# A speech joint network's forward and backward pass: 16 rows of x columns with a copied halo, x rows in one tile, and sums over u two halves at a time

## The chip, the core and the metric

The kernel runs on one core of a Trainium2 chip. The core has TensorE (PE, matmuls and their weight loads), VectorE (DVE), ScalarE (ACT), GpSimd (POOL) and SyncE (SP, which here only issues DMAs), each with its own instruction queue that is worked off in order. SBUF is the on-chip memory, PSUM the place where matmuls leave their sums. The metric is the device time of one launch in microseconds (us).

## The reference

Two batches of 16000 frames with 256 channels go through two convolutions of three taps, each followed by GELU and by taking every second frame, so that 4000 frames are left in each batch. A joint network adds each of them to each of 8 rows of `g` and takes tanh. The kernel returns the output and the gradients of all seven inputs, in bfloat16.

```python
h = sum(einsum("btc,cd->btd", xp[:, i:i+T], w1[i]) for i in range(3))   # xp: x padded by one frame at both ends
h = gelu(h)[:, ::2, :]
f = sum(einsum("btc,cd->btd", hp[:, i:i+T1], w2[i]) for i in range(3))
f = gelu(f)[:, ::2, :]
fe = einsum("btd,de->bte", f, w_f)
ge = einsum("bud,de->bue", g, w_g)
j = tanh(fe[:, :, None, :] + ge[:, None, :, :])
out = einsum("btud,dv->btuv", j, w_o)                                    # [2, 4000, 8, 256]
# returned: out and, from grad_out, the gradients of x, w1, w2, g, w_f, w_g, w_o
```

## The kernel before

The 8000 frames that are left (both batches one after the other) are cut into 17 chunks: one of 256, fifteen of 512, one of 64. A chunk of 512 lies in SBUF as 4 blocks of 128 columns: frame 4p + a of the chunk is column p of block a. Channels are in two halves of 128 (`KT` = 2, index `kt`, `mt` or `d2`). The batches meet inside chunk 8, whose operations therefore come in two segments.

A chunk goes through three stages.

- `stage_a` (lines 532 to 591): x arrives with channels on partitions in tile `XC`, which has one slot. A chunk of 512 needs 17 rows of columns: 16 of its own and row 0, the frame before each group of 16 (the halo), which is row 16 of the column to its left. `load_xc` (line 395) fetches them with four transposing DMAs of 5, 4, 4 and 4 rows. Convolution, GELU and its derivative follow (`conv_gelu`, line 494) for odd frames (`HTo`, `G1o`), even frames (`HTe`, `G1e`) and the second layer (`FT`, `G2`). In `conv_gelu` PE writes PSUM tiles `ps`; ACT makes `g_sq` (L505) and the GELU (L507); DVE makes `g_s` (L510) and so gives the PSUM tile back; L519 to L529 make the derivative. Then `FE` = f w_f in its transposed layout, and the row layouts `FER`, `HRo`, `HRe`, `FR` for the weight gradients.
- `stage_j` (line 622): for each of four pairs of u, ACT makes `JT` = tanh(FE + ge) (L638) and DVE and ACT the same in rows, `JR`, from `FER` and the broadcast rows `GEB` (L662, L667). PE makes the output from JT, the gradient of w_o from JR and `GO` (into `GWO`), and from `GOT` (grad_out transposed) the gradient of the joint sum into `ps`. `JSQ` is the square of JT. For each u and half DVE computes (JSQ - 1) x ps into `NGZ` (L709, with a sum along the row for the gradient of ge), and adds it to `ZS` (L724); for the last u the sum goes to `NGFE` (L722). `NGZ` is a 512-wide fp32 tile for one half and has two slots.
- `stage_de` (line 767): the backward pass of the two layers (`GF`, `GHe`, `GHo`, with their halos copied by POOL, L377 and L383), the row layouts `NFR`, `GFR`, `GHeR`, `GHoR` (class "rows", three slots), the weight gradients (`wgrad`, added to accumulators in L763) and the gradient of x (`GX`). `load_x` (line 444) brings x in rows for the gradient of w1, in two tiles of 9 rows for a chunk of 512.

While chunk k is in `stage_j`, chunk k+1 is in `stage_a` and chunk k-1 in `stage_de`. The order on each engine isn't that of the text: a planner (`Flow.issue`, line 107) walks through a simulated time, and at each step places the operation that can start first, by costs written at each operation and a due time (`at`, or `F.now`). An operation that needs a new tile (`new=`) is placed only when its class has a free slot; the classes and their numbers of slots are in lines 295 to 298, and most give slots out in the order of the text. `ps` has 7 slots in PSUM. The matmul of GOT and WOT asks for its `ps` tile and for its `NGZ` tile (line 690). The planner's order is fixed at build time; on the chip semaphores keep the dependences.

All DMAs but a few at the start are issued on SP's queue, where an issue waits for its own data and holds what is behind it.

Of the kernel before, what the change touches and what calls it, by code (L numbers as in the profile page):

```python
# [220 lines left out]
def kernel(  # L221
# [38 lines left out]
    sizes.append(NP - sum(sizes))  # L260
    assert sum(sizes) == NP

    TRANS = (0,)

    class Chunk:
# [100 lines left out]
    def zero(ap, w, new=(), at=None):  # L366
        op("POOL", 150.0, lambda e: nc.gpsimd.memset(ap(), 0.0), w=w, new=new, at=at)
# [17 lines left out]
    def row_ap(t, row, step, m, n):  # L385
        return bass.AP(tensor=t.tensor, offset=t.offset + row * D, ap=[[step * D, m], [1, n * D]])
# [8 lines left out]
    def load_xc(k, at, behind=()):  # L395
        c = chunks[k]
        A, Pw = c.A, c.Pw
        XC = st[k]["XC"] = buf("xc", [P, 4 * NB + 1, KT, P], BF16, "XC")
        cuts = [1, 4 * A + 1] if c.first else [0] + [4 * n + 1 for n in range(1, A + 1)]
        for n, (lo, hi) in enumerate(zip(cuts, cuts[1:])):  # L400
            dma("SP", lambda lo=lo, hi=hi: XC[:, lo:hi, :, :Pw].rearrange("p r k c -> p (r k) c"),
                lambda lo=lo, hi=hi: row_ap(x_, 4 * c.c0 - 1 + lo, 4 * A, Pw, hi - lo), r=[], w=[(XC, ("m", n))],
                bytes_=Pw * (hi - lo) * D * 2 * 1.3, new=[XC] if n == 0 else [], transpose=True, at=at, behind=behind, sub="xc")
        if c.first:
            op("POOL", 330.0, lambda e: nc.gpsimd.tensor_copy(out=XC[:, 0, :, 1:Pw], in_=XC[:, 4 * A, :, 0:Pw - 1]),
               r=[(XC, ("m", 0))], w=[(XC, "h")], at=at)
            zero(lambda: XC[:, 0, :, 0:1], [(XC, "h")], at=at)
        if c.px is not None:
            zero(lambda: XC[:, 0, :, c.px:c.px + 1], [(XC, ("m", 0))], at=at)

    def load_go(k, up, at, after=()):
        c = chunks[k]
# [31 lines left out]
    def load_x(k, at, after=()):  # L444
        c = chunks[k]
        A = c.A
        tiles = []
        for h in range((A + 1) // 2):
            nb = min(2, A - 2 * h)
            nr = 4 * nb + 1  # L450
            X = buf("xc" if c.last else "x", [P, 9, D], BF16, "X")
            row = 4 * c.c0 - 3 + 8 * h
            lo, new = 0, [X]
            if c.first and h == 0:
                op("POOL", 150.0, lambda e, X=X: nc.gpsimd.memset(X[0:1, 0:3], 0.0), w=[(X, "a")], new=new, at=at, after=after)
                new = []
                dma("SP", lambda X=X, nr=nr: X[0:1, 3:nr], lambda nr=nr: x[0:1, 0:nr - 3, :], r=[], w=[(X, "b")],
                    bytes_=(nr - 3) * 512, at=at, after=after)
                dma("SP", lambda X=X, nr=nr: X[1:16, 0:nr].rearrange("p f d -> p (f d)"),
                    lambda row=row, nr=nr: row_ap(x_, row + 4 * A, 4 * A, 15, nr), r=[], w=[(X, "c")],  # L460
                    bytes_=15 * nr * 512, at=at, after=after)
                lo = 16
            rd = []
            if c.last and h == 0:
                p0 = c.Pw // 32 * 32
                zero(lambda X=X, p0=p0: X[p0:c.Pw + 1], [(X, "z")], new=new, at=at)
                new, rd = [], [(X, "z")]
                dma("SP", lambda X=X: X[c.Pw:c.Pw + 1, 0:3], lambda: x[B - 1:B, T - 3:T, :], r=rd, w=[(X, "b")],
                    bytes_=1536, at=at, after=after)
            dma("SP", lambda X=X, lo=lo, nr=nr: X[lo:c.Pw, 0:nr].rearrange("p f d -> p (f d)"),  # L470
                lambda row=row, lo=lo, nr=nr: row_ap(x_, row + 4 * A * lo, 4 * A, c.Pw - lo, nr),
                r=rd, w=[(X, "m")], bytes_=(c.Pw - lo) * nr * 512, new=new, at=at, after=after)
            tiles.append(X)
        return tiles
# [147 lines left out]
    def stage_j(k, t0, dt, GEB):  # L622
# [5 lines left out]
        def pair(up):  # L628
# [51 lines left out]
            for step in range(4):  # L680
# [21 lines left out]
                if first:  # L702
                    Z, zap = (ZS, d2), lambda d2=d2: ZS[:, d2, :W]
                else:
                    Z, zap = NGZ, lambda NGZ=NGZ: NGZ[:, :W]

                def stt(e, d2=d2, ps=ps, u=u, zap=zap, JSQ=JSQ):
                    for _, lo, hi, si in c.segs:
# [3 lines left out]
                            accum_out=NGP[:, d2, u, si:si + 1])  # L712
                op("DVE", sum(c_dve((s[2] - s[1]) * A) + 6 for s in c.segs), stt,
                   r=[JSQ, ps], w=[Z, (NGP, (d2, u, k))])
                if not first:
                    if fin_ and d2 == 0:
                        S["NGFE"] = buf("ngfe", [P, NB, KT, P], BF16, "NGFE")

                    def zadd(e, d2=d2, NGZ=NGZ, fin_=fin_):
                        a, b = ZS[:, d2, :W], NGZ[:, :W]  # L720
                        if fin_:
                            nc.vector.tensor_tensor(out=S["NGFE"][:, 0:A, d2, :Pw], in0=fl(a, A), in1=fl(b, A), op=ALU.add)  # L722
                        else:
                            nc.vector.tensor_tensor(out=a, in0=a, in1=b, op=ALU.add)  # L724
# [42 lines left out]
    def stage_de(k, t0, dt):  # L767
# [158 lines left out]
                    put(Pw, Pw + 1, 0, 3)  # L926
        for i in range(KK):
            def xl(da):
                return lambda a, m, d2: X[a // 2][:m, 4 * (a % 2) + da, d2 * P:(d2 + 1) * P]
# [3 lines left out]
            wgrad(ACC1, i, lambda i=i: ACC1[:, i],  # L933
                  [(xl(i), rr(GHoR), c.sblk, X + [GHoR]),
                   (xl(i + 2), he, c.sblk, [GHeR] + ([GHzR] if GHzR is not None else []))], out_2[i])
            tick()

    def store(dst, src, r, scale=None):
# [73 lines left out]
    xh = st[0]["XC"].log[-1][0]  # L1012
# [25 lines left out]
    def wt(dst, src, n, at, behind):  # L1038
        dma("SP", lambda: dst[:], lambda: src, r=[], w=[dst], bytes_=n * 131072, transpose=True, at=at, behind=behind)


    def part(k):
        return str(k) if k < 4 else "e" if k >= NG - 2 else "s"
# [7 lines left out]
    for k in range(NG + 1):  # L1051
        c = chunks[min(k, NG - 1)]
        t0, Wk = (c.t0, float(c.W)) if k < NG else (float(NP), 300.0)
        if k < NG:
            F.stage = part(k)
            for up in range(1 if c.last else UP):
                load_go(k, up, t0 + Wk * (up / UP - 0.7), [xh] if k == 0 else [])
                load_got(k, up, t0 + Wk * (up / UP - 0.5))
        F.stage = part(k)
        if k + 1 < NG:  # L1060
            load_xc(k + 1, t0 - Wk * 0.3, [st[0]["GOT"][1].log[0][0]] if k == 0 else [])
        if k == 0:
            fr = st[1]["XC"].log[-1][0]
# [55 lines left out]
```

## Time and profile before

| what | before |
|---|---|
| median of 3 runs | 806.55 us (805.66 to 807.43) |
| the profiled execution | 807.35 us |
| its span, first to last instruction | 805.6 us |
| granted TensorE clock | 1.000 |
| PE busy | 780.1 us (97%), 5916 matmuls |
| DVE busy | 727.5 us (90%), 1626 instructions |
| ACT busy | 732.0 us (91%), 1175 instructions |
| POOL busy | 61.4 us (8%), 179 instructions |
| moved by DMA | 180.86 MB |

The span runs from the first to the last instruction; what the profiled execution has over it (1.75 us) lies outside. A busy time is the time in which at least one instruction of the engine was running, and a group's mean is the length of one instruction, which may overlap the next one's start. A wait is counted at the engine that stood still, with what released it.

### The profile page before, as it was taken

What the parts mean: (1) busy time and instruction counts of PE and PEld (TensorE: products, weight loads), DVE (VectorE), ACT (ScalarE), POOL (GpSimd) and SP (SyncE); (2) the same over time, 40 slices, a digit from 0 to 9 for tenths busy, and PEclk for the clock granted to TensorE, in tenths of its full rate; (3) what the DMA queues carried; (4) which work ended last, traced back from release to release, by engine and by line L of the source; (5) the groups of instructions that cost most, each with busy time, mean ns of one, the idle gap of its engine ahead of it and who ended that gap; (6) DMA issues with size and microseconds to landing.
All of it is one profiled execution on the core that took longest, in us unless ns stands there. A gap on an engine that the chain in (4) does not pass through costs nothing. (4 is left out here: it accounts for less than half of the span.)

```text
span 805.6 us, 16179 instructions
## 1 busy us (share of the span) xinstructions
PE 780.1 (97%) x5916; PEld 558.7 (69%) x5916; DVE 727.5 (90%) x1626; ACT 732.0 (91%) x1175; POOL 61.4 (8%) x179
## 2 busy tenths in 40 slices
PE   7879999999999999999999999999999999999996
PEld 6546668576675766767677686776767767677865
DVE  4799999998998989989899898998989989899974
ACT  5999999999999989998999999999999999998742
POOL 2100000100001001010000101000010000103010
PEclk9999999999999999999999999999999999999999
DMA  9998999999999999998999999999999999997984
GB/s 191 208 203 209 218 277 220 234 237 232 240 219 222 251 236 222 214 239 208 239 232 210 262 218 231 221 247 254 217 225 243 241 212 221 239 249 190 249 168 130
DMA packets 387940, 180.86 MB, mean 225 GB/s; under 512 B 311794, under 2 KB 379668, under 8 KB 387860
## 3 DMA queue, kind: packets, MB, share of 16 engines
q1 hardware_dynamic: 386916, 179.16, 99.0%
q8 instruction: 46, 0.75, 0.4%
q10 hardware_dynamic: 784, 0.39, 0.2%
q0 software_dynamic: 160, 0.27, 0.1%
q14 instruction: 34, 0.28, 0.1%
HBM read 52.40 MB, written 50.34 MB: 128 GB/s over the span
## 5 line engine op out<-in xcount | busy, mean ns | idle before, releaser
L638 ACT ACTIVATE JT<-FE,GE 128x512 bf16<-128x512 bf16 (+4 forms) x288 | 182.4, 690 | 0.2
L709 DVE SCALAR_TENSOR_TENSOR NGZ<-JSQ,ps 128x512 f32<-128x512 bf16 (+3 forms) x252 | 150.1, 608 | 1.0 <-PE ps L335 0.6
L335 PE MATMUL ps<-WO,JT 128*128 128x256 bf16 (+1 forms) x1008 | 146.2, 273 | 2.7 <-DVE NGZ L709 1.7
L335 PE MATMUL ps<-GOT,WOT 128*128 128x512 bf16 (+2 forms) x544 | 146.3, 362 | 2.2 <-DVE g_s L510 1.0
L344 ACT CAST OUT_SB<-ps 128x512 bf16<-128x512 f32 (+1 forms) x207 | 122.7, 606 | 18.3 <-PE ps L335 18.1
L667 ACT ACTIVATE JR<-JR 128x1024 bf16<-128x1024 bf16 (+1 forms) x124 | 130.7, 1071 | 5.7 <-DVE JR L662 5.6
L335 PEld LDWEIGHTS <-JT 128*128 128x128 bf16 (+1 forms) x1008 | 98.1, 98 | 51.5 <-issue 4.5
L696 ACT ACTIVATE JSQ<-JT 128x1024 bf16<-128x1024 bf16 (+2 forms) x124 | 127.3, 1027 | 7.2 <-DVE NGZ L709 5.1
L335 PE MATMUL GWO<-GO,JR 128*128 128x256 bf16 (+1 forms) x1008 | 130.7, 273 | 1.5 <-ACT JR L344 0.8
L724 DVE TENSOR_TENSOR ZS<-ZS,NGZ 128x512 f32<-128x512 f32 (+2 forms) x204 | 129.1, 638 | 0.4
L335 PEld LDWEIGHTS <-JR 128*128 128x128 bf16 (+1 forms) x1008 | 97.5, 98 | 23.5 <-ACT JR L667 2.6
L510 DVE SCALAR_TENSOR_TENSOR g_s<-g_sq,ps 128x512 bf16<-128x512 bf16 (+2 forms) x102 | 65.1, 640 | 41.7 <-ACT HTo L507 41.1
L335 PEld LDWEIGHTS <-W 128*128 128x128 bf16 x612 | 58.5, 99 | 61.0 <-issue 4.6
L335 PE MATMUL ps<-XC,W 128*128 128x512 bf16 (+2 forms) x408 | 85.5, 367 | 1.9 <-DMA XC<-in_x_dram 1.2
L662 DVE TENSOR_TENSOR JR<-FER,GEB 128x1024 bf16<-128x1024 bf16 (+1 forms) x124 | 83.3, 678 | 3.0 <-PE GWO L335 2.3
L335 PEld LDWEIGHTS <-X 128*128 128x128 bf16 (+1 forms) x756 | 73.8, 98 | 9.7 <-issue 0.4
L763 DVE TENSOR_TENSOR ACC<-ACC,ps 128x512 f32<-128x512 f32 x90 | 60.1, 680 | 19.3 <-PE ps L335 18.8
L335 PE MATMUL ps<-W1T,GHo 128*128 128x256 bf16 (+1 forms) x378 | 72.2, 273 | 0.2
L335 PEld LDWEIGHTS <-WOT 128*128 128x128 bf16 x544 | 51.9, 98 | 29.1 <-issue 4.1
L335 PE MATMUL ps<-W1T,GHe 128*128 128x256 bf16 (+1 forms) x376 | 71.8, 273 | 0.0
L505 ACT ACTIVATE g_sq<-ps 128x512 bf16<-128x512 f32 (+2 forms) x102 | 59.6, 586 | 10.2 <-PE ps L335 10.0
L346 ACT ACTIVATE GX_SB<-ps 128x512 bf16<-128x512 f32 (+1 forms) x101 | 60.1, 616 | 5.6 <-PE ps L335 4.6
(137 smaller groups left out, 1109.8 us busy)
## 6 DMA issues: line engine op xcount, KB each, us to landing
GO<-in_grad_out_dram SPq DMA_DIRECT2D x60, 512.0 KB, 5.0
out_dram<-OUT_SB SPq DMA_DIRECT2D x60, 512.0 KB, 5.1
X<-in_x_dram SPq DMA_DIRECT2D x30, 576.0 KB, 5.4
out_dram<-GX_SB SPq DMA_DIRECT2D x30, 512.0 KB, 5.0
GO<-in_grad_out_dram SPq DMA_DIRECT2D x5, 256.0 KB, 4.2
GOT<-GO SPq DMA_TRANSPOSE x65, 4.9
out_dram<-OUT_SB SPq DMA_DIRECT2D x4, 256.0 KB, 3.1
XC<-in_x_dram SPq DMA_TRANSPOSE x62, 4.7
```

The costliest lines, as they stand in the source:

```text
L335: nc.tensor.matmul(ps_ap, lhsT=lhsT, rhs=rhs, start=start, stop=stop)
L344: nc.scalar.copy(out=dst(), in_=src())
L346: nc.scalar.activation(out=dst(), in_=src(), func=ACT.Copy, scale=scale)
L505: op("ACT", c_act(W, True), lambda e, mt=mt, ps=ps: nc.scalar.activation(out=sq[:, 0:A, mt, :Pw], in_=fl(ps[:, :W], A), func=ACT.Square, s ...
L510: op("DVE", c_dve(W), lambda e, mt=mt, ps=ps: nc.vector.scalar_tensor_tensor(out=s[:, 0:A, mt, :Pw], in0=sq[:, 0:A, mt, :Pw], scalar=1.0, ...
L638: nc.scalar.activation(out=fl(JT[:, j, mt, :W], A)[:, :, lo:hi], in_=FE[:, 0:A, mt, lo:hi], func=ACT.Tanh, bias=GE[:, b, mt, 2 * up + j:2 ...
L662: op("DVE", c_dve(n * 2 * D, 0.5), lambda e, lo=lo, n=n, m=m, JR=JR: nc.vector.tensor_tensor(out=JR[:m, 0:n], in0=S["FER"][:m, lo:lo + n]. ...
L667: op("ACT", c_act(n * 2 * D), lambda e, n=n, m=m, JR=JR: nc.scalar.activation(out=JR[:m, 0:n], in_=JR[:m, 0:n], func=ACT.Tanh), r=[JR], w= ...
L696: nc.scalar.activation(out=JSQ[:, :, :W], in_=JT[:, j, :, :W], func=ACT.Square)
L709: nc.vector.scalar_tensor_tensor(out=fl(zap(), A)[:, :, lo:hi], in0=fl(JSQ[:, d2, :W], A)[:, :, lo:hi], scalar=1.0, in1=fl(ps[:, :W], A)[: ...
L724: nc.vector.tensor_tensor(out=a, in0=a, in1=b, op=ALU.add)
L763: op("DVE", c_dve(512), lambda e: nc.vector.tensor_tensor(out=acc_ap().rearrange("p k d -> p (k d)"), in0=acc_ap().rearrange("p k d -> p ( ...
```

## The change

- `load_xc`: a chunk's transposing DMAs now bring rows 1 to 16 in four pieces of 4 rows. Row 0 is made in SBUF by POOL: 127 columns copied from row 16 of the same tile, and column 0 from `XCh`, a small tile of two slots into which POOL copies the last column of row 16 for the next chunk. The first chunk did the first of these copies already.
- `load_x`: x rows come in one tile of 17 rows with one DMA (first chunk: three, last chunk: two); the class "x" has one slot of 17 rows where it had two of 9.
- Sums over u: `NGZ` holds both halves (1024 wide, two slots). The two L709 instructions of a u write its halves, and one add of 1024 columns follows the second. For the last u two adds of 512 remain, in one operation behind the second half.
- `geb` gets a second slot. Classes with fewer slots: `fe` 2 to 1, `got` 4 to 3, `hro` 2 to 1, `rows` 3 to 2, `x` 2 to 1.
- `F.shift` is set to an empty table, which is what it was by default, and the operations that waited for "the last entry of XC's log" now name the last XC DMA itself.

```diff
-    for name, n in (("xc", 1), ("hto", 2), ("hte", 1), ("ft", 1), ("g1o", 2), ("g1e", 2), ("g2", 2), ("fe", 2),
-                    ("fer", 2), ("gsq", 2), ("gs", 2), ("jt", 3), ("go", 3), ("got", 4), ("out", 3), ("jr", 3),
-                    ("hro", 2), ("hre", 2), ("fr", 2), ("jsq", 2), ("ngz", 2), ("ngfe", 1), ("gf", 2), ("gho", 1),
-                    ("ghe", 1), ("rows", 3), ("x", 2), ("gx", 3), ("ghh", 2), ("geb", 1)):
+    for name, n in (("xc", 1), ("hto", 2), ("hte", 1), ("ft", 1), ("g1o", 2), ("g1e", 2), ("g2", 2), ("fe", 1),
+                    ("fer", 2), ("gsq", 2), ("gs", 2), ("jt", 3), ("go", 3), ("got", 3), ("out", 3), ("jr", 3),
+                    ("hro", 1), ("hre", 2), ("fr", 2), ("jsq", 2), ("ngz", 2), ("ngfe", 1), ("gf", 2), ("gho", 1),
+                    ("ghe", 1), ("rows", 2), ("x", 1), ("gx", 3), ("ghh", 2), ("xch", 2), ("geb", 2)):
...
-        cuts = [1, 4 * A + 1] if c.first else [0] + [4 * n + 1 for n in range(1, A + 1)]
+        cuts = [1, 4 * A + 1] if c.first else [1] + [4 * n + 1 for n in range(1, A + 1)]
...
+        end = (XC, ("m", len(cuts) - 2))
+        op("POOL", 330.0, lambda e: nc.gpsimd.tensor_copy(out=XC[:, 0, :, 1:Pw], in_=XC[:, 4 * A, :, 0:Pw - 1]),
+           r=[end], w=[(XC, "h")], at=at)
         if c.first:
...
             zero(lambda: XC[:, 0, :, 0:1], [(XC, "h")], at=at)
+        else:
+            xh_ = st[k - 1]["XCh"]
+            op("POOL", 200.0, lambda e: nc.gpsimd.tensor_copy(out=XC[:, 0, :, 0:1], in_=xh_[:]), r=[xh_], w=[(XC, "h")], at=at)
...
+        if not c.last:
+            xh2 = st[k]["XCh"] = buf("xch", [P, KT, 1], BF16, "XC_halo")
+            op("POOL", 200.0, lambda e: nc.gpsimd.tensor_copy(out=xh2[:], in_=XC[:, 4 * A, :, Pw - 1:Pw]),
+               r=[end], w=[xh2], new=[xh2], at=at)
...
-        for h in range((A + 1) // 2):
-            nb = min(2, A - 2 * h)
-            nr = 4 * nb + 1
-            X = buf("xc" if c.last else "x", [P, 9, D], BF16, "X")
-            row = 4 * c.c0 - 3 + 8 * h
+        nr = 4 * A + 1
+        X = buf("xc" if c.last else "x", [P, 4 * NB + 1, D], BF16, "X")
+        row = 4 * c.c0 - 3
...
-                NGZ = buf("ngz", [P, CW], FP32, "NGZ") if u else None
-                op("PE", c_pe([W] * KT), gj, r=[GOT, WOT], w=[ps], new=[ps, NGZ] if u else [ps])
+                if u and d2 == 0:
+                    NGZ = buf("ngz", [P, KT, CW], FP32, "NGZ")
+                op("PE", c_pe([W] * KT), gj, r=[GOT, WOT], w=[ps], new=[ps, NGZ] if u and d2 == 0 else [ps])
...
-                if not first:
-                    if fin_ and d2 == 0:
+                if not first and d2 == KT - 1:
+                    if fin_:
...
-                    def zadd(e, d2=d2, NGZ=NGZ, fin_=fin_):
-                        a, b = ZS[:, d2, :W], NGZ[:, :W]
+                    def zadd(e, NGZ=NGZ, fin_=fin_):
+                        a, b = ZS[:, :, :W], NGZ[:, :, :W]
...
-                    op("DVE", c_dve(W), zadd, r=[(ZS, d2), NGZ], w=[(S["NGFE"] if fin_ else ZS, d2)],
-                       new=[S["NGFE"]] if fin_ and d2 == 0 else [])
+                    op("DVE", KT * c_dve(W) if fin_ else c_dve(KT * W), zadd, r=[ZS, NGZ],
+                       w=[(S["NGFE"], 0), (S["NGFE"], 1)] if fin_ else [ZS], new=[S["NGFE"]] if fin_ else [])
```

More of the change, by code (lines that the diff above doesn't have):

```diff
@@ L261 @@
     assert sum(sizes) == NP
+    SHIFT = {}
     TRANS = (0,)
@@ L446, in load_x @@
         A = c.A
-        tiles = []
-        for h in range((A + 1) // 2):
-            nb = min(2, A - 2 * h)
-            nr = 4 * nb + 1
-            X = buf("xc" if c.last else "x", [P, 9, D], BF16, "X")
-            row = 4 * c.c0 - 3 + 8 * h
[L453 to L473, printed above, removed]
@@ L474, in load_x @@
-        return tiles
+        nr = 4 * A + 1
+        X = buf("xc" if c.last else "x", [P, 4 * NB + 1, D], BF16, "X")
+        row = 4 * c.c0 - 3
+        lo, new = 0, [X]
+        if c.first:
+            op("POOL", 150.0, lambda e, X=X: nc.gpsimd.memset(X[0:1, 0:3], 0.0), w=[(X, "a")], new=new, at=at, after=after)
+            new = []
+            dma("SP", lambda X=X, nr=nr: X[0:1, 3:nr], lambda nr=nr: x[0:1, 0:nr - 3, :], r=[], w=[(X, "b")],
+                bytes_=(nr - 3) * 512, at=at, after=after)
+            dma("SP", lambda X=X, nr=nr: X[1:16, 0:nr].rearrange("p f d -> p (f d)"),
+                lambda row=row, nr=nr: row_ap(x_, row + 4 * A, 4 * A, 15, nr), r=[], w=[(X, "c")],
+                bytes_=15 * nr * 512, at=at, after=after)
+            lo = 16
@@ new lines, in load_x @@
+        rd = []
+        if c.last:
+            p0 = c.Pw // 32 * 32
+            zero(lambda X=X, p0=p0: X[p0:c.Pw + 1, 0:nr], [(X, "z")], new=new, at=at)
+            new, rd = [], [(X, "z")]
+            dma("SP", lambda X=X: X[c.Pw:c.Pw + 1, 0:3], lambda: x[B - 1:B, T - 3:T, :], r=rd, w=[(X, "b")],
+                bytes_=1536, at=at, after=after)
+        dma("SP", lambda X=X, lo=lo, nr=nr: X[lo:c.Pw, 0:nr].rearrange("p f d -> p (f d)"),
+            lambda row=row, lo=lo, nr=nr: row_ap(x_, row + 4 * A * lo, 4 * A, c.Pw - lo, nr),
+            r=rd, w=[(X, "m")], bytes_=(c.Pw - lo) * nr * 512, new=new, at=at, after=after)
@@ L476, in rows @@
+        return X
     def rows(k, cls, name, SRC, lo, n, r, at=None, pe=0):
@@ L704, in pair @@
                 else:
-                    Z, zap = NGZ, lambda NGZ=NGZ: NGZ[:, :W]
+                    Z, zap = (NGZ, d2), lambda NGZ=NGZ, d2=d2: NGZ[:, d2, :W]
                 def stt(e, d2=d2, ps=ps, u=u, zap=zap, JSQ=JSQ):
@@ L714, in pair @@
                    r=[JSQ, ps], w=[Z, (NGP, (d2, u, k))])
-                if not first:
-                    if fin_ and d2 == 0:
+                if not first and d2 == KT - 1:
+                    if fin_:
                         S["NGFE"] = buf("ngfe", [P, NB, KT, P], BF16, "NGFE")
-                    def zadd(e, d2=d2, NGZ=NGZ, fin_=fin_):
-                        a, b = ZS[:, d2, :W], NGZ[:, :W]
+                    def zadd(e, NGZ=NGZ, fin_=fin_):
+                        a, b = ZS[:, :, :W], NGZ[:, :, :W]
                         if fin_:
-                            nc.vector.tensor_tensor(out=S["NGFE"][:, 0:A, d2, :Pw], in0=fl(a, A), in1=fl(b, A), op=ALU.add)
+                            for d in range(KT):
+                                nc.vector.tensor_tensor(out=S["NGFE"][:, 0:A, d, :Pw], in0=fl(ZS[:, d, :W], A),
+                                                        in1=fl(NGZ[:, d, :W], A), op=ALU.add)
                         else:
                             nc.vector.tensor_tensor(out=a, in0=a, in1=b, op=ALU.add)
-                    op("DVE", c_dve(W), zadd, r=[(ZS, d2), NGZ], w=[(S["NGFE"] if fin_ else ZS, d2)],
-                       new=[S["NGFE"]] if fin_ and d2 == 0 else [])
+                    op("DVE", KT * c_dve(W) if fin_ else c_dve(KT * W), zadd, r=[ZS, NGZ],
+                       w=[(S["NGFE"], 0), (S["NGFE"], 1)] if fin_ else [ZS], new=[S["NGFE"]] if fin_ else [])
                 for tb, m in c.blk:
@@ L933, in stage_de @@
             wgrad(ACC1, i, lambda i=i: ACC1[:, i],
-                  [(xl(i), rr(GHoR), c.sblk, X + [GHoR]),
-                   (xl(i + 2), he, c.sblk, [GHeR] + ([GHzR] if GHzR is not None else []))], out_2[i])
+                  [(xl(i), rr(GHoR), c.sblk, [X, GHoR]),
+                   (xl(i + 2), he, c.sblk, [X, GHeR] + ([GHzR] if GHzR is not None else []))], out_2[i])
             tick()
@@ L1039, in wt @@
         dma("SP", lambda: dst[:], lambda: src, r=[], w=[dst], bytes_=n * 131072, transpose=True, at=at, behind=behind)
+    F.shift = SHIFT
     def part(k):
@@ L1062 @@
         if k == 0:
-            fr = st[1]["XC"].log[-1][0]
+            fr = st[1]["XCl"]
             wt(WFT, w_f[:, :], 1, W0 * 0.6, [fr])
```

10 lines of the change are left out of this document (4 added, 6 removed).

## The prediction

> **What bounds the kernel now.** I read the page's busy shares first, then the busy time by stretches, the chain of waits on TensorE (PE), the groups by form, and last the timeline around one chunk change. From the page, PE's busy tenths in 40 slices last:
>
> ```profile
> PE 780.1 (97%) x5916; PEld 558.7 (69%) x5916; DVE 727.5 (90%) x1626; ACT 732.0 (91%) x1175; POOL 61.4 (8%) x179
> PE   7879999999999999999999999999999999999996
> ```
>
> PE is busy in every slice but the first three and the last. The stretches (us, then busy time and instructions of each engine):
>
> ```profile
> 32.00:104.00 72.00, 65.08 (x449) 41.68 (x448) 71.10 (x161) 70.32 (x110) 6.03 (x19) 1.00 1.01 214
> 104.00:700.00 596.00, 590.77 (x4424) 423.48 (x4423) 550.70 (x1168) 567.82 (x877) 39.36 (x116) 1.00 1.03 231
> 700.00:805.60 105.60, 97.36 (x839) 73.69 (x837) 88.96 (x241) 71.84 (x142) 11.36 (x28) 1.00 0.80 200
> ```
>
> Columns are PE, weight loads, VectorE (DVE), ScalarE (ACT), GpSimd (POOL). So there are two regimes. From 32 to 104 us DVE is busy for 71.1 of 72 us and PE for only 65.1: DVE sets the pace. From 104 to 700 us PE does, idle for 5.2 of 596 us. What ends its waits there (total us, times, longest), from the chain of waits between 100 and 700 us:
>
> ```profile
> PE ps L335 <- DVE g_s L510: 2.3, 6, 0.6
> PE ps L335 <- ACT FT L507: 1.0, 3, 0.4
> PE ps L335 <- DVE NGZ L709: 0.6, 3, 0.2
> ```
>
> No row has a DMA in it. In 32 to 104 us the same view gives 5.1 us of PE waits ended by DVE (g_s 1.9 and 0.7, NGZ 1.7, GF 0.6, GHe 0.2; nine waits). A change to DVE counts only through these 8.0 us; a change to DMA counts only if it makes a wait that is not there today.
>
> **The change, part by part.** First the sums over u. The groups by form (count, busy us, mean ns) and two adds in a row in the timeline (start, us):
>
> ```profile
> L724 DVE TENSOR_TENSOR ZS<-ZS,NGZ 128x512 f32<-128x512 f32 x180 | 121.9, 681 | 0.1
> ...
> 214.45 1.28 DVE L724 TENSOR_TENSOR ZS<-ZS,NGZ 128x512 f32<-128x512 f32 x2
> ```
>
> Two adds back to back take 1.28 us though one lasts 0.68, so the second starts 0.60 us after the first. The 256-wide form lasts 418 ns, so an element costs (681 - 418)/256 = 1.03 ns and a 1024-wide add lasts 0.68 + 512 x 1.03 = 1.21 us. One merged add saves 1.28 - 1.21 = 0.07 us. L724 stands 204 times (6 values of u, 2 halves, 17 chunks), so 102 merges save 7.1 us of DVE's 727.5. The last add of a chunk (L722) stays two instructions; both now wait for the second half, but at 769.07 and 793.01 us both already stand behind it: nothing. [...]
>
> What of 7.1 us reaches PE? In 32 to 104 us DVE is the bound and has 20 of these adds: 10 x 0.07 = 0.7 us, all of it. Between 100 and 700 us the nine waits above each have about one merge before them in the same unbroken DVE stream: 9 x 0.07 = 0.6 us. The pair tile also changes the order: the planner may place the matmul of GOT and WOT only when an NGZ slot is free, and with two 512-wide slots that ties it to the add of the u just before; with two slots of a pair it may run one u further ahead. No row shows that. Its bounds are a gain of what is left of those waits (2.9 - 0.6 = 2.3 us) and the loss of rival C; I take 1.0 us of gain, since the nearest rows (the waits on NGZ and g_s) are just this matmul waiting for DVE. Together: 2.3 us.
>
> Next, the 48 new POOL copies (16 chunks, three each). The halo copy of the same shape lasts 394 ns and the one-column copies some 190 ns, so POOL gets 16 x 0.78 = 12 us more on 61. Where they hide: in the chunk whose x columns are read from 198.9 us the last transpose is issued by 189.3 and should have landed near 192.5, and POOL does nothing between 161.4 (G1o's halo) and 194.29 (GF's). Queued behind them are GF's and GHe's halos (to 198.5) and HTo's (203.0), for which the next matmuls of those chunks wait. If the cover went (columns that land late), two of HTe's six taps and these halos would stand still for the delay, 0.8 us a chunk for the copies alone; PE's waits on POOL in the old run are one of 0.7 us, so I take 0. But they are not free for DVE:
>
> ```profile
> 160.23 0.80 POOL L377 COPY G1o<-G1o 128x254 bf16<-128x254 bf16 x1 [6.21 <-DVE G1o L529]
> 160.69 0.62 DVE L521 TENSOR_SCALAR g_sq<-g_sq 128x1024 bf16<-128x1024 bf16 x1
> ...
> L521 DVE TENSOR_SCALAR g_sq<-g_sq 128x1024 bf16<-128x1024 bf16 x45 | 21.5, 478 | 0.5
> L525 DVE TENSOR_SCALAR g_sq<-g_sq 128x1024 bf16<-128x1024 bf16 x45 | 18.8, 418 | 0.1
> ```
>
> The copy takes 0.80 instead of 0.39 us and the tensor_scalar under it 0.62 instead of 0.41; over the run L521 loses 45 x 60 ns = 2.7 us to such meetings, and L527 (431 ns) 0.6. That is 3.3 us for some 113 copies, 0.03 each, so 48 more cost DVE 1.4 us; at the rate at which DVE time reached PE above, 2.3/7.1, that is 0.5 us; I take 0.3, since the new copies come outside the tensor_scalar bursts.
>
> Fewer bytes: 15 rows of x columns and 15 of x rows (64 KB each) less of 180.86 MB, and 15 issues less on SyncE's queue. PE waits for no DMA after start: 0, bounds 0 and 0.
>
> Fewer slots cost only where the old order used the last slot. GOT: no transpose was issued sooner than 4.1 us after the last read of the tile three before it: 0. X: one 17-row load may start when the last X is read; the old loads started at least 5.9 us after that, and the second of each pair landed some 16 to 20 us before use: 0. HRo: now loaded where its successor was (515.34 us), over 40 us before its read: 0; the last one moves from 751.2 to 781.9 us, lands within 5 us, read at 796.4: 0. Rows of the gradients and FE:
>
> ```profile
> 508.85 3.16 SPq L359 DMA_TRANSPOSE GHeR<-GHe  x1
> 511.09 1.04 PE L335 MATMUL ps<-NFR,FR 128*128 128x256 bf16 x8
> ...
> 413.40 1.15 ACT L344 CAST FE<-ps 128x512 bf16<-128x512 f32 x2
> 420.13 0.92 ACT L638 ACTIVATE JT<-FE,GE 128x160 bf16<-128x160 bf16 x2
> 424.26 0.78 ACT L638 ACTIVATE JT<-FE,GE 128x512 bf16<-128x512 bf16 x1
> ```
>
> With two "rows" slots GHeR waits for NFR's reads (512.1) and GHoR for GFR's (515.2): three us later, read at 526. Behind them on SyncE's queue stand HRo and HRe, needed a chunk later, and the next GOT (519.2), read at 533.8. At the end GHoR moves from 777.7 to 781.9 us; with its longest landing time of 6.5 us it would be 2.4 us late for the read at 786.0, with its median of 3.5 in time: bounds 0 and 2.4, I take 0. FE with one slot is written after the last read by JT. In most chunks it was (3 to 19 us after); in four it wasn't: 73.8 against 84.4, 119.6 against 120.8, 413.4 against 421.0 (lines above), 461.7 against 461.9. There FE's copy (0.65), the transposes (0.6) and FER's copy (1.0) follow 84.4 or 421.0 and end near 87 and 424; the next JT ran at 85.6 and 424.3, the first add of FER for the new chunk at 90.3 and 428.9. 0, bounds 0 and 3 us. The second slot for broadcast ge rows: those of the second batch were written at 406 us, when the first had long been read: 0.
>
> Sum: -2.3 + 0.3 = -2.0 us. The profiled execution took 807.35 us (span 805.6), 0.8 above the median of 806.55: 807.35 - 2.0 = 805.35, and 804.55 against the median.
>
> **The rivals.** B, nothing reaches PE: it has 97% of the span, and 7 us of DVE may just become DVE idle time (DVE has 45 us of it between 104 and 700 us). Against it: the stretch from 32 to 104 us. 806.5 us, no change (0.2%, 1.6 us, is about what a measurement can tell). C, slower: the long add stands in front of the release. DVE works in order, and PE waits for a PSUM slot that g_s or NGZ gives back; an add of 1.13 us (to the next start) instead of 0.60 ahead of it makes that wait 0.53 us longer. The eighteen waits counted above would give 9.5 us, half of them 4.8: 807.35 + 4.8 - 0.8, about 811.4 us. More matmuls of GOT run ahead and hold the seven PSUM slots at the same time, which speaks for it; that two adds now mostly follow one another (214.45) speaks against. It decides once it lengthens more than four waits (4 x 0.53 = 2.1), which is all the gain. D, POOL's copies hold DVE: if each of the 48 meets a tensor_scalar, at 0.4 us (at 160.69 it was 0.2, and the longest L521 is 1.12 us, 0.7 above the usual), DVE loses 19 us and gains 7, and 12 x 2.3/7.1 = 3.9 us reach PE: 807.35 + 3.9 - 0.8, about 810.4 us. For it the 0.80 us row; against it that the three tensor_scalars have 60 us of DVE's 806, so few will meet. [...]
>
> **How the numbers follow.** Forecast 0.42 (own range 798 to 805), B 0.20, C 0.28, D 0.10. So faster by over 0.2% 0.42, within it 0.20, slower 0.38. The low end has all 8.0 us of PE's waits on DVE gone: 806.55 - 8.0, about 798. The high end is C with three quarters of its waits: 807.35 + 7.2 - 0.8, about 814; the 3 us of FE and 2.4 us of the tail lie within it.
>
> **What would show it.** Right: L724 102 times at some 1.2 us, DVE busy near 721 us, 20 loads of X where there were 35, PE's waits ended by DVE below 2.9 us in 100 to 700. B: the same, with PE's idle time unchanged. C: these waits longer and an L724 in front of them. D: L521 and L527 above 478 and 431 ns. Wrong altogether: waits of PE on DMA, on FE or FER, or a longer stretch before 104 us.

## The result, and the profile after

| what | before | after |
|---|---|---|
| median | 806.18 us (805.66 to 807.43, 4 runs) | 800.42 us (797.41 to 800.94, 4 runs) |
| ratio of the runs | | 0.9917, interval 0.9900 to 0.9935 |
| the profiled execution | 807.35 us, span 805.6 | 797.41 us, span 795.6 |
| sum of PE's waits in the chain of waits, whole span | 18.7 us (11.2 ended by DVE) | 14.3 us (2.2 ended by DVE) |

The kernel became 0.8% faster, some 5.8 us where 2.0 were predicted. The ratio, taken over all runs, comes to 6.7 us of 806. The profiled execution of after is its fastest by 2.8 us and that of before one of its slowest, so the spans overstate the gain: 10.0 us against 5.8.

The page after, with engine totals and PE's busy tenths in 40 slices:

```profile
PE 774.8 (97%) x5916; PEld 559.2 (70%) x5916; DVE 725.2 (91%) x1535; ACT 720.7 (91%) x1164; POOL 67.5 (8%) x227
PE   7989899999999999999999999999999999999996
```

DVE lost 91 instructions but only 2.3 us (727.5 to 725.2); ACT, whose work the change doesn't touch, lost 11.3 us. Some of its work has moved to DVE. FE's copies out of PSUM, for one, were 26 on ACT and 4 on DVE in chunks of 512, and are 18 and 12 now. The planner chooses the engine of such a copy; it has made another plan.

The busy time by stretches (us, then busy time and instructions of PE, weight loads, DVE, ACT, POOL; clock, DMA share, GB/s):

```profile
32.00:104.00 72.00, 66.13 (x454) 42.72 (x452) 70.14 (x153) 70.45 (x112) 9.26 (x25) 0.98 1.03 216
104.00:700.00 596.00, 592.54 (x4458) 426.64 (x4457) 557.21 (x1120) 560.58 (x871) 43.53 (x154) 1.00 1.02 230
700.00:795.60 95.60, 88.73 (x782) 68.86 (x780) 76.46 (x202) 65.31 (x131) 8.73 (x26) 0.98 0.86 209
```

From 104 to 700 us PE does 34 matmuls more and is idle for 3.5 us where it was 5.2; DVE is busy for 6.5 us *more* there, not less, and ACT for 7.2 less. What ends PE's waits between 100 and 700 us is a single row:

```profile
PE psb L489 <- ACT FE L345: 3.2, 9, 0.8
```

All waits on g_s and NGZ (2.9 us before) are gone. The row on FE was 0.4 us before: FE's copy now comes late and the transposes into `psb` stand for it. FE has one slot now; that alone doesn't make the wait, since e7 below has one slot too and no such row. Between 32 and 104 us the same view has 0.3 us ended by DVE where it had 5.1, but 4.3 us on JR where it had 0.4:

```profile
PE GWO L336 <- ACT JR L672: 4.3, 3, 1.7
```

Of the 10.0 us between the two spans, 4.4 lie in these named waits. PE's busy time, for the same 5916 matmuls, is another 5.3 us shorter (780.1 to 774.8). Short stalls hide in it, because a matmul of 512 columns is shown as 379 ns long while the next one starts some 216 ns after it: starts of successive matmuls lie 300 to 600 ns apart 33 times in before and 16 times in after.

The groups by form (count, busy us, mean ns), and two instructions of the timeline (start, us) around one merged add:

```profile
L732 DVE TENSOR_TENSOR ZS<-ZS,NGZ 128x1024 f32<-128x1024 f32 x90 | 109.9, 1221 | 0.5
L526 DVE TENSOR_SCALAR g_sq<-g_sq 128x1024 bf16<-128x1024 bf16 x45 | 19.1, 425 | 0.4
L406 POOL COPY XC<-XC 128x254 bf16<-128x254 bf16 x16 | 8.3, 518 | 408.8 <-PE ps L336 190.6 <-DMA XC<-in_x_dram 162.2 <-PE GWO L336 30.9
```

```profile
212.04 1.23 DVE L732 TENSOR_TENSOR ZS<-ZS,NGZ 128x1024 f32<-128x1024 f32 x1
213.17 0.70 DVE L667 TENSOR_TENSOR JR<-FER,GEB 128x1024 bf16<-128x1024 bf16 x1
```

The merged add lasts 1.22 us and the next instruction starts 1.13 us after it, as was worked out. The tensor_scalar that was to be hit by POOL's copies (L526, L521 before) fell from 478 to 425 ns although POOL has 48 copies more.

### The profile page after: what moved, and what is told of

Its sections match the earlier page's. It is cut to its first block, busy times and chain, and to the rows that moved or that the text cites. A ratio compares the mean times of both kernels' runs of the same rounds, so it can differ in the third digit from the quotient of the medians.

```text
span 795.6 us, 16104 instructions
## 1 busy us (share of the span) xinstructions
PE 774.8 (97%) x5916; PEld 559.2 (70%) x5916; DVE 725.2 (91%) x1535; ACT 720.7 (91%) x1164; POOL 67.5 (8%) x227
## 4 chain that ended last, share of the span: by engine, by line
PE 55%; ACT 24%; DVE 14%; issue 4%; DMA 3%; SPq 0%; DVEq 0%; ACTq 0%
PE ps L336 45%; PE GWO L336 8%; ACT JT L643 5%; ACT JR L672 4%; ACT JSQ L702 4%; ACT OUT_SB L345 3%; DVE g_s L515 3%; DVE NGZ L715 2%; ACT GX_SB L347 2%; ACT g_sq L510 1%; DVE ZS L732 1%; DMA GO<-in_grad_out_dram 1%; PE psb L489 1%; DMA out_dram<-OUT_SB 1%; DVE ACC L771 1%
## 5 line engine op out<-in xcount | busy, mean ns | idle before, releaser
L643 ACT ACTIVATE JT<-FE,GE 128x512 bf16<-128x512 bf16 (+4 forms) x288 | 190.7, 723 | 0.3 <-PE ps L336 0.3
L715 DVE SCALAR_TENSOR_TENSOR NGZ<-JSQ,ps 128x512 f32<-128x512 bf16 (+3 forms) x252 | 152.3, 613 | 1.6 <-PE ps L336 1.5
L336 PE MATMUL ps<-WO,JT 128*128 128x256 bf16 (+1 forms) x1008 | 150.0, 274 | 0.7 <-ACT JT L643 0.6
L336 PE MATMUL ps<-GOT,WOT 128*128 128x512 bf16 (+2 forms) x544 | 149.3, 363 | 0.4 <-DMA GOT<-GO 0.4
L672 ACT ACTIVATE JR<-JR 128x1024 bf16<-128x1024 bf16 (+1 forms) x124 | 136.2, 1101 | 12.8 <-DVE JR L667 12.8
L345 ACT CAST OUT_SB<-ps 128x512 bf16<-128x512 f32 (+1 forms) x215 | 132.7, 629 | 12.7 <-PE ps L336 12.5
L732 DVE TENSOR_TENSOR ZS<-ZS,NGZ 128x1024 f32<-128x1024 f32 (+2 forms) x102 | 115.8, 1135 | 0.5
L771 DVE TENSOR_TENSOR ACC<-ACC,ps 128x512 f32<-128x512 f32 x90 | 60.8, 684 | 20.1 <-PE ps L336 19.3
L510 ACT ACTIVATE g_sq<-ps 128x512 bf16<-128x512 f32 (+2 forms) x102 | 62.2, 610 | 8.6 <-PE ps L336 6.0
```

The source lines that it names most:

```text
L336: nc.tensor.matmul(ps_ap, lhsT=lhsT, rhs=rhs, start=start, stop=stop)
L345: nc.scalar.copy(out=dst(), in_=src())
L510: op("ACT", c_act(W, True), lambda e, mt=mt, ps=ps: nc.scalar.activation(out=sq[:, 0:A, mt, :Pw], in_=fl(ps[:, :W], A), func=ACT.Square, s ...
L643: nc.scalar.activation(out=fl(JT[:, j, mt, :W], A)[:, :, lo:hi], in_=FE[:, 0:A, mt, lo:hi], func=ACT.Tanh, bias=GE[:, b, mt, 2 * up + j:2 ...
L672: op("ACT", c_act(n * 2 * D), lambda e, n=n, m=m, JR=JR: nc.scalar.activation(out=JR[:m, 0:n], in_=JR[:m, 0:n], func=ACT.Tanh), r=[JR], w= ...
L715: nc.vector.scalar_tensor_tensor(out=fl(zap(), A)[:, :, lo:hi], in0=fl(JSQ[:, d2, :W], A)[:, :, lo:hi], scalar=1.0, in1=fl(ps[:, :W], A)[: ...
```

## The experiments

Each ratio is against the kernel before on the same chip: 805.95 us for e1 to e4, 807.13 for e5 to e8, 806.86 for e9 to e12. For the first four there were three theories: **relief** (the merged adds free DVE, and so PE), **order** (any part of the change gives the planner another sequence, which is faster or slower by itself) and **loads** (fewer bytes and shorter loads let chunks start sooner).

### The parts one by one: e1 to e4

e1 is before with the paired NGZ and the merged add (got 3, to make space); e2 is before with the smaller classes fe, got, hro and rows; e3 is before with the x columns in 16 rows and the copied halo; e4 is before with the x rows in one tile.

```diff
# e1
-                NGZ = buf("ngz", [P, CW], FP32, "NGZ") if u else None
+                if u and d2 == 0:
+                    NGZ = buf("ngz", [P, KT, CW], FP32, "NGZ")
# e2
-    ("fe", 2), ... ("got", 4), ... ("hro", 2), ... ("rows", 3)
+    ("fe", 1), ... ("got", 3), ... ("hro", 1), ... ("rows", 2)
# e3
-        cuts = [1, 4 * A + 1] if c.first else [0] + [4 * n + 1 for n in range(1, A + 1)]
+        cuts = [1, 4 * A + 1] if c.first else [1] + [4 * n + 1 for n in range(1, A + 1)]
# e4
-            X = buf("xc" if c.last else "x", [P, 9, D], BF16, "X")
+        X = buf("xc" if c.last else "x", [P, 4 * NB + 1, D], BF16, "X")
```

> The kernel before with the sums over u of the change alone (pair tile NGZ, one add of 1024 columns), and three GOT slots instead of four to make room, which leave TensorE's order as it was. Theory 'VectorE relief': the 7 us that VectorE saves and the freer order of GOT's matmuls are the gain, so 800 to 802 us. Theory 'order': any part gives the planner another sequence, and its time lies anywhere within some 5 us of before; 801 to 811. Theory 'x loads': the gain is in the x columns and rows, so 806 here.

> The kernel before with fe 1, got 3, hro 1 and rows 2 slots alone. Theory 'VectorE relief': nothing gained, 806 or a little slower. Theory 'order', in its form that fewer slots pace the planner into an order that repeats from chunk to chunk: 800 to 803. Theory 'x loads': 806.

> The kernel before with the x columns in 16 rows and the halo row copied by GpSimd alone. Theory 'VectorE relief': 806 to 808, since GpSimd's copies meet VectorE's work. Theory 'order': within 5 us of before, either sign. Theory 'x loads': 800 to 803.

> The kernel before with x rows in one tile of 17 alone. Theory 'VectorE relief': 806. Theory 'order': within 5 us of before, either sign. Theory 'x loads': 803 to 805, with the rest of the gain in the x columns.

| part alone | median us | ratio, interval |
|---|---|---|
| e1 sums over u | 804.37 | 0.9973, 0.9964 to 0.9983 |
| e2 fewer slots | 807.80 | 1.0015, 1.0001 to 1.0029 |
| e3 x columns | 799.85 | 0.9919, 0.9904 to 0.9933 |
| e4 x rows | 803.85 | 0.9972, 0.9958 to 0.9986 |

The x columns alone give as much as the whole change, and they are the part that the prediction had priced at zero. Relief, which said 806 to 808 us for e3, is off there by 6 us. By the ratios (times 806 us) the single effects come to -2.2 + 1.2 - 6.5 - 2.3 = -9.8 us, and the whole change to -6.7: the parts do not add, which speaks for order. e2 was a miss of the order theory's number (it expected a gain there); e1 falls short of relief's 800 to 802. Order and loads were still open for e3, since its plan also differs from that of before, and for e4, whose time fits both theories and which was not taken apart further.

### The x columns' plan without the x columns: e5

The kernel computes and moves what before does; the planner alone is told another price and another predecessor.

```diff
-                bytes_=Pw * (hi - lo) * D * 2 * 1.3, ...
+                bytes_=Pw * (min(4, hi - lo) if not c.first else hi - lo) * D * 2 * 1.3, ...
-    xh = st[0]["XC"].log[-1][0]
+    xh = st[0]["XCl"]                      # the last DMA of XC; the same for fr
```

> The kernel before with nothing changed in what it computes or moves: only two entries of the planner are those of the new x columns. The first transposing DMA of a chunk is priced as 4 rows instead of 5 (it still brings 5), and the first loads of the start wait for the last x-column DMA instead of the last entry of the log. TensorE's order is then that of the kernel with the x columns alone in 84% of its places. Order theory (the x columns gain by the other order that the planner makes): 799 to 802 us, DVE busy unchanged near 728. Byte theory (the 15 rows fewer and the copy on POOL give the gain on the chip): 806, as before.

801.88 us, ratio 0.9948 (0.9932 to 0.9964). One price and one predecessor in a planner give 4.2 us on the chip, nearly two thirds of e3's gain by the ratios. DVE's busy time, expected unchanged near 728 us, came out at 733.7: in the other plan DVE has 12 instructions more and ACT 12 fewer. Loads, which said 806, can't be all of it.

### The merged add taken out of after: e6

```diff
-                            nc.vector.tensor_tensor(out=a, in0=a, in1=b, op=ALU.add)
+                            for d in range(KT):
+                                nc.vector.tensor_tensor(out=ZS[:, d, :W], in0=ZS[:, d, :W], in1=NGZ[:, d, :W], op=ALU.add)
```

> The kernel after, with each 1024-column add issued as two adds of 512 columns while the planner still prices one of 1024, so that every engine's order is that of after; it leaves out only the 0.07 us that a merge saves, 90 full-size merges, about 6.3 us of DVE. Relief theory (the merged add gives a good part of the gain): 803 to 806 us. Order theory: 800.4 to 801.5 us, at most the 2 us that the first prediction gave to the merge, and DVE waits of PE between 100 and 700 us return by less than 2 us.

799.92 us, ratio 0.9917 (0.9904 to 0.9931), against 0.9917 for after. The totals of its page:

```profile
PE 777.3 (97%) x5916; PEld 560.1 (70%) x5916; DVE 731.4 (92%) x1637; ACT 721.1 (90%) x1164; POOL 68.5 (9%) x227
```

The merges do save DVE 731.4 - 725.2 = 6.2 us, as predicted (90 full ones at 0.069), and none of it can be seen in the time, which lies a little below even the order theory's range. Relief, which said 803 to 806, falls. The two intervals together leave room for a worth of up to some 1.8 us. In the profiles PE's waits ended by DVE are 1.4 us longer without the merge (3.6 against 2.2), all its waits 0.5 us (14.8 against 14.3).

### After with the old x columns: e7, and a planner's constant: e8

```diff
# e7, against after
-        cuts = [1, 4 * A + 1] if c.first else [1] + [4 * n + 1 for n in range(1, A + 1)]
+        cuts = [1, 4 * A + 1] if c.first else [0] + [4 * n + 1 for n in range(1, A + 1)]
# e8, against before: c_dve, the planner's price of a DVE instruction
-    return 66.0 + 1.042 * n * f
+    return 67.0 + 1.042 * n * f
```

> The kernel after with the old loads of x columns: 17 rows by four transposing DMAs of 5, 4, 4 and 4 rows, no halo copy on POOL but the first chunk's. If the x columns carry the gain by themselves: 804 to 806 us, near the sums alone (804.4) or the x rows alone (803.9). If the other parts now give it as well (any part brings an order of the better kind): 799 to 802. The wait of the g_s that frees a PSUM tile should return in the first case: DVE-ended waits of PE between 100 and 700 us of 2 to 4 us.

> The kernel before with one number of the planner changed: the fixed cost it gives a DVE instruction, 67 ns instead of 66. Nothing is computed or moved otherwise; only the order differs (from the 3,508th equal place on). It shows how far an order alone moves the time. Order theory: anywhere from 800 to 810 us, and off 806 by more than 1 us. If the order matters little: 805.5 to 806.5.

e7: 805.89 us, ratio 0.9993 (0.9979 to 1.0006). All the other parts together, without the x columns, show no gain in the time. But e7 ran at lower granted clocks (0.990 to 0.997) than before on the same chip (0.995 to 1.000). At 0.995 its three executions have spans of 803.9 to 804.2 us, the four of before 805.8 to 806.2, so some 2 us may hide there. Its waits of PE between 104 and 700 us, the first rows:

```profile
PE ps L336 <- DVE g_s L507: 4.2, 7, 0.8
PE GWO L336 <- ACT JR L664: 3.0, 4, 1.3
```

The waits on g_s are back, though the merged adds are still there. e8: 806.21 us, ratio 0.9993 (0.9983 to 1.0003), a miss for the order theory, which expected to see the time move by more than 1 us. Its order is another one almost from the start: PE's weight loads first differ from those of before at the 369th, and are the same in 3654 of 5916 places. Another order isn't always another time; it depends on which.

### Loads and order crossed: e9 and e10

These two separate what e3 had together. The sequence in which the planner places operations, with the engine and the slots of each, was taken down once for before and once for e3, written into the other kernel as a list, and followed there in place of the choice:

```diff
-            best = None
-            for e, lst in avail.items():
...
+            i, e, fixed = order[at]       # next operation, its engine, its slots
+            o = by_id[i]
...
+                at += 1
```

> The kernel before, with its own loads of x columns (17 rows, no halo copy on POOL), but the order of every engine's operations, and the choice of slots, written out from the kernel with the x columns alone (the copies that it doesn't have are left out; the one zeroing at the seam of the batches stands a few places earlier). Order theory: 798.5 to 801.5 us, as with the x columns alone (ratio 0.992). Load theory (what the chip does less or sooner gives the gain): 805 to 807. Half and half: some 803.

> The other corner: 16 rows of x columns and POOL's halo copies, but TensorE, VectorE and ScalarE in exactly the order of the kernel before, with its choice of slots. The copies stand on POOL where the planner's clock has them ready. Order theory: 805.5 to 808 us, no gain, and perhaps a little loss by the copies. Load theory: 799 to 801.

| | order of before | order of e3 |
|---|---|---|
| old loads (17 rows) | before: 1 | e9: 0.9927 (0.9912 to 0.9941), 800.36 us |
| new loads (16 rows, halo copied) | e10: 1.0009 (0.9998 to 1.0021), 807.57 us | e3: 0.9919 (0.9904 to 0.9933) |

The orders were carried over exactly: in the traces DVE's, ACT's and the weight loads' instructions of e10 stand in the sequence of before, all 8717 of them, and those of e9 in the sequence of e3. The clock isn't the cause either: executions with a granted clock of 0.998 or more have spans of 797.7 to 798.9 us in e9, 803.6 to 804.1 in e10 and 803.8 to 805.7 in before on the same chip.

The gain goes with the order and not with the loads. The new loads in the old order are not faster; the old loads in the new order are as fast as e3 within the intervals. So the 0.8% of the x columns is the planner's other sequence (with its choice of engines and slots), shown. That the 0.8% of the whole change is the same thing is an inference from e3, e6 and e7: after's own order was not put into a kernel with the old loads, and the x rows and the slots were not crossed.

Where it sits can be read by comparing e10 with e9. Inserted code shifts the lines: g_s is L659 in e10 and L646 in e9 (L510 before), NGZ L858 and L845 (L709), NGFE L871 and L858 (L722). The chain of waits over the whole span, e10 first:

```profile
PE ps L471 <- DVE g_s L659: 3.6, 8, 0.7
PE ps L471 <- ACT FT L656: 2.3, 5, 1.0
PE ps L471 <- DVE NGZ L858: 2.1, 5, 1.0
PE ps L471 <- DVE NGFE L871: 2.1, 3, 1.1
```

```profile
PE ps L471 <- DVE NGZ L845: 1.8, 4, 1.0
PE GWO L471 <- ACT JR L803: 1.5, 4, 0.6
PE ps L471 <- ACT FT L643: 1.4, 2, 1.0
...
PE ps L471 <- DVE NGFE L858: 1.1, 1, 1.1
...
PE ps L471 <- DVE g_s L646: 1.0, 5, 0.3
```

And the first and the long stretch, e10 and then e9:

```profile
0.00:32.00 32.00, 27.43 (x218) 20.12 (x219) 18.16 (x60) 23.82 (x54) 6.24 (x22) 1.00 1.02 213
...
104.00:700.00 596.00, 590.84 (x4427) 423.99 (x4426) 550.99 (x1170) 567.52 (x875) 48.65 (x150) 1.00 1.02 230
```

```profile
0.00:32.00 32.00, 28.35 (x217) 21.07 (x218) 20.24 (x61) 21.47 (x49) 5.20 (x18) 0.95 1.05 206
...
104.00:700.00 596.00, 592.44 (x4432) 424.48 (x4431) 561.32 (x1190) 563.22 (x871) 38.18 (x117) 1.00 1.05 235
```

All rows of the waits sum to 17.7 us in e10 and 13.1 in e9: 4.6 of the 5.2 us between their spans (805.2 and 800.0) lie in named waits. By stretches (0 to 32, 32 to 104, 104 to 700, the rest) they go from 4.4, 5.8, 4.3 and 3.1 to 3.7, 5.6, 2.7 and 1.1 us. The largest fall is g_s, from 3.6 to 1.0 (a further row of g_s, 0.7 us on `psb`, stands in both), then NGFE and FT. DVE is *busier* in the faster kernel, by 10.3 us in the long stretch and 2.1 in the first 32 us (the same stretches, in which the faster kernel gets further), and by 7.6 over the whole (734.9 against 727.3); ACT is busy for 4.3 us less in the long one. Written into the two orders are 1322 operations on DVE and 1159 on ACT against 1336 and 1145: 14 change sides on balance. In the groups by form DVE's copies of OUT_SB go from 45 to 52, of FR from 3 to 7, of FER from 6 to 8, and its JSQ from 12 to 9.

What PE waits for is not how much DVE has to do but what stands ahead of the one instruction that gives a PSUM slot back. One place in the same chunk shows it, e10 first, then e9 (start, us):

```profile
257.54 0.68 DVE L672 TENSOR_TENSOR g_sq<-g_sq,HTe 128x1024 bf16<-128x1024 bf16 x1
258.14 0.68 DVE L659 SCALAR_TENSOR_TENSOR g_s<-g_sq,ps 128x512 bf16<-128x512 bf16 x1
...
258.87 0.59 PE L471 MATMUL ps<-GOT,WOT 128*128 128x512 bf16 x2 [0.47 <-DVE g_s L659]
```

```profile
256.42 0.69 DVE L646 SCALAR_TENSOR_TENSOR g_s<-g_sq,ps 128x512 bf16<-128x512 bf16 x1
...
258.94 0.68 DVE L659 TENSOR_TENSOR g_sq<-g_sq,HTe 128x1024 bf16<-128x1024 bf16 x1
```

In e10 the product with HTe, which frees no PSUM slot, stands before the two g_s of `FT`. Their input is ready at 257.77 us, when its GELU ends, but the first g_s starts at 258.14, and PE waits for it. In e9 the product stands behind both; the first g_s starts 0.03 us after its GELU, and PE doesn't wait there. Whether the other places are of this kind, and whether the 14 moved operations or the sequence itself does more, is open.

e10 also answers the question on POOL's copies without a change of order (groups by form):

```profile
L670 DVE TENSOR_SCALAR g_sq<-g_sq 128x1024 bf16<-128x1024 bf16 x45 | 21.5, 479 | 0.5
L513 POOL COPY G1o<-G1o 128x254 bf16<-128x254 bf16 x16 | 10.6, 662 | 84.1 <-DVE G1o L678 84.1
L542 POOL COPY XC<-XC 128x254 bf16<-128x254 bf16 x16 | 8.7, 544 | 50.5 <-PE ps L471 50.2 <-DMA XC<-in_x_dram 0.3
```

L670 is L521 of before: 479 ns against 478. The new copies are themselves lengthened (544 ns against 394 undisturbed), but the tensor_scalar is not, nor is DVE as a whole (727.3 us busy, 727.5 before). Of the 48 new copies only two ran beside a tensor_scalar, the same one of 423 ns at 42.15 us. In e9, with the new order, this group lasts 444 ns without the copies, and in after 425 with them. How often the two meet is set by the order, too.

### Two candidates: e11 and e12

e11 is after with the old slots for fe, hro, rows and geb; e12 is before with both x parts and nothing else.

```diff
# e11, against after
-    ("fe", 1), ... ("hro", 1), ... ("rows", 2), ... ("geb", 2)
+    ("fe", 2), ... ("hro", 2), ... ("rows", 3), ... ("geb", 1)
# e12, against before: the diffs of e3 and e4 together
```

> The kernel after with the old slots: fe 2, hro 2, rows 3 and one slot for the broadcast ge rows (got stays 3 and x 1, for space). The waits of TensorE for the copy of FE (3.2 us between 100 and 700) should be gone. If they cost what they last: 797 to 798.5 us, faster than after. If this part too acts through the order alone: within 799 to 804, with no relation to these waits.

> The kernel before with both x parts (16 rows of columns with copied halo, x rows in one tile), and neither the sums nor the slots. If the single gains add up (0.9919 and 0.9972): 797.5 us, faster than after. If each only draws another order: 799 to 802, no better than the x columns alone.

e11: 798.68 us, ratio 0.9901 (0.9888 to 0.9914). It has the lowest median of all kernels here, 0.2% under after by the ratios and between the ranges of its two theories. But the intervals overlap, and it ran at higher granted clocks (0.998 to 0.999, after 0.994 to 0.997): that it beats after is open. Its waits between 104 and 700 us:

```profile
PE ps L336 <- DVE ACC L771: 0.4, 1, 0.4
PE ps L336 <- DVE FR L350: 0.3, 1, 0.3
PE ps L336 <- ACT GX_SB L347: 0.2, 1, 0.2
```

FE's 3.2 us are gone and PE waits for 0.9 us in all. By the ratios the time falls by 1.3 us only (0.0016 of 806); waits on g_s, NGZ and ZS (2.9, 2.1 and 0.8 us) come up between 32 and 104 us, where after had 0.3 on g_s. e12: 802.01 us, ratio 0.9945 (0.9931 to 0.9959), at the edge of the range given for another order: with a second "gain" added, the x columns do no better than alone (0.9919). Single gains that come from a plan can't be summed.

PE's waits, summed over the whole span of each profile, against the ratio:

| kernel | ratio | waits us | of them ended by DVE |
|---|---|---|---|
| e2 | 1.0015 | 18.1 | 11.1 |
| e10 | 1.0009 | 17.7 | 10.6 |
| before | 1 | 18.7 | 11.2 |
| e7, e8 | 0.9993 | 20.1, 19.3 | 8.5, 11.9 |
| e1, e4 | 0.9973, 0.9972 | 15.8, 17.8 | 8.1, 11.2 |
| e5, e12 | 0.9948, 0.9945 | 15.6, 13.7 | 9.9, 7.1 |
| e9, e3 | 0.9927, 0.9919 | 13.1, 13.5 | 7.0, 6.9 |
| e6, after | 0.9917, 0.9917 | 14.8, 14.3 | 3.6, 2.2 |
| e11 | 0.9901 | 13.5 | 8.7 |

Every kernel above 803 us has 15.8 us or more, every one below at most 15.6. It is the sum of the waits that goes with the time; the part ended by DVE, by which the prediction steered, goes with it less well. The sum doesn't rank neighbours (e12 has less of it than e6 and is slower), and each profile is of a single execution.

## Why the prediction was right, and where its steps failed

The direction and the place were right: faster, through PE's waits on DVE, which fell from 11.2 to 2.2 us while no wait on DMA stands in the long stretch. The low end of the range, "all 8.0 us of PE's waits on DVE gone", is close to what the profile shows for 32 to 700 us (0.3 us left of 8.0; 7.5 us on FE and JR came instead). The size was off by 3.8 us, and the reason given was the wrong one: the merged add was to give 1.3 us and the pair tile 1.0, and most of the gain came from a part priced at nothing. That the time fell into the range is therefore luck as far as the reasons go; kernels with other selections of the same parts, and so with other plans, came out at 802 us (e12) and 806 (e7). One of the prediction's own signs of being "wrong altogether" did appear, too, waits of PE on FE (3.2 us), and the time fell all the same.

- **Merged adds, 0.07 us each and 7.1 us of DVE.** Right: 1221 ns, 1.13 us to the next start, 6.2 us between e6 and after for the 90 full ones, 69 ns a merge.
- **"0.7 + 0.6 reach PE".** Not seen: e6 shows no loss of time without the merge. Its intervals allow up to some 1.8 us, so 1.3 us is not excluded; zero is the nearest value.
- **"Freer order, 1.0 us".** The term was of the right kind and too narrow. It was given to the NGZ pair alone, with bounds from the waits that this pair meets. e1, the sums alone, gains 2.2 us, as much as the 2.3 us foretold for them; whether by order or by relief was not separated there. In the whole change it is the x columns that make the difference (e7 without them 0.9993).
- **"Fewer bytes: 0, bounds 0 and 0".** As a statement on the loads it held: e10 has them and is at 1.0009. As the price of that part of the change it was the step that failed, by 6.5 us. Each part but NGZ was priced with the order of before held fixed; but the edit also changed two inputs of the planner, the price of the first transposing DMA and what the first loads wait for, and e5 shows that these alone are worth 4.2 us. An edit with no cost on the chip was taken for one with no effect.
- **POOL's copies, 0.3 us.** Not contradicted as a cost (e10: at most 0.2% and not distinct from nothing). Rival D falls: the 48 copies did not lengthen the tensor_scalar in the old order (479 against 478 ns), because they hardly met one, as the prediction argued against D; in after's order it got shorter (425). The row that D leaned on was read in part only: the copy at 160.23 us started under an add of ZS and NGZ (160.09 to 160.77), before the tensor_scalar at 160.69.
- **Slots, 0 each.** X, HRo and rows made no wait of PE, and GOT one of 0.4 us; GHoR landed a median of 3.3 us after its issue. FE was the exception, a little above its bounds of 0 and 3: nine waits, 3.2 us. e2, the smaller slots together, costs 0.15%. The second slot for the ge rows was priced at 0 and not tried alone.
- **Rival B** had its half: of the DVE time that the merges save nothing is seen in the time (e6). The waits went for another reason. **Rival C** falls: between 100 and 700 us no wait on NGZ or g_s is left to lengthen.
- **Signs.** L732 stands 102 times, the 90 of full size at 1.22 us, and X is loaded 20 times, as foretold; DVE at 725.2 instead of 721 was the sign that the plan had moved copies between engines.

## What to carry to other kernels

Where a planner with prices fixes the order at build time, an edit has two effects: what it does on the chip, and what it does to the plan; take down the order and cross the two before crediting the edit. Gains that came from the plan did not add here, and they may be reached or lost through a number that changes nothing on the chip. On an engine that is not the bound, look at what stands ahead of the instruction that gives a buffer back, not at its total: DVE was busy for 7.6 us more in the faster of e9 and e10.

## What the runs showed of the hardware

The granted TensorE clock differs between executions of one kernel on one chip, in short stretches: 0.95 in 32 to 104 us of e7's profile, 0.95 in the first 32 us of e9's. e7's twelve executions go with it: spans of 805.6 to 807.4 us at a mean clock of 0.990, 803.4 to 804.2 at 0.993 to 0.995, 802.3 at 0.997. That is 5 us within one kernel, as much as the whole change, and a reason to read 0.5% from the interval and not from two profiles. In before the relation is looser (805.8 us at 1.000, 804.5 at 0.998).

That 48 POOL copies should leave the DVE instructions they might meet as they were, and be lengthened themselves (544 ns for 394), had not been expected. Single meetings in e10 show when it happens. Ten of the 16 copies of 254 columns lasted 391 to 397 ns; beside them DVE ran nothing, or instructions with an operand in PSUM (such as L858; one copy began in the last 12 ns of a tensor_tensor). The other six lasted 592 to 888 ns, and each of them started while DVE ran a tensor_tensor with both inputs in SBUF (`JR` from `FER` and `GEB` five times, the add of ZS and NGZ once). Those six tensor_tensors lasted 415 to 691 ns, their usual lengths. The other way round, one add that started 0.28 us after such a copy lasted 884 ns instead of 685. In the trace of before the copies of `GHe` show the same: seven of the 16 of 254 columns started under an add of ZS and NGZ and lasted 0.73 to 0.74 us, the adds 0.68 to 0.69; the other nine lasted 0.39 to 0.40 us. In these meetings the instruction that started second was the one that was lengthened; why it is so, no run shows.
